# Attention loads issued later, first keys earlier, and weight conversion steps moved in a fused attention and two-layer MLP kernel

## The chip, the cores and the metric

The kernel runs on one NeuronCore of a Trainium2 chip. The metric is device time in microseconds of one execution. 1076.02 us is the median of three runs before the change. A profile was taken of one more execution. The engines are called as the profile calls them: PE (matmul, PEld for its weight loads), DVE (VectorE), ACT (ScalarE), POOL (GpSimd), SP (SyncE, which here issues nearly all loads and stores; SPq is its queue).

## The reference

Chunked attention with a few memory keys, then two products of gated linear layers. Cut to what matters:

```python
batch, n_heads, seq, head_dim = (4, 8, 768, 64); n_mem = 8
chunk, left_ctx, right_ctx = (32, 16, 8)
for c in range(seq // chunk):
    k_full = concat([mem_k, k[l_start:r_end]]); v_full = concat([mem_v, v[l_start:r_end]])
    a = softmax(scale * q_c @ k_full.T)
    out[c] = a @ v_full
x = out as (3072 tokens, 512)
a = x @ w1; b = x @ w2              # 512 -> 1024
x = ((a * b) @ w3) @ w_out          # 1024 -> 1024 -> 512
y = ((x @ w_a) * (x @ w_b)) @ w_out2   # 512 -> 1536 -> 512
```

## The kernel before, in words

The work is one long stream of matmuls on PE in four stages, written out in an order that Python fixes; the other engines run what is queued to them, in order.

Stage 1 multiplies w3 by w_out once (tiles wps, lines 566 to 605), in two halves of 16 steps g; each step is two matmuls of 128 x 512, and four banks of results are evicted to wo by w_evict at the end of a half (ACT writes the high part, DVE the low part). The weights come as 64-bit words, and are made into 32-bit floats on the way: SP loads a raw block (w_load, line 350; w3a and w3b blocks of 1 MiB, w12 blocks of 0.5 MiB), ACT scales its two halves (w_scale, line 366, two instructions, L372 and L373), DVE adds them (w_bits, L377 and L378), and for w12 blocks ACT writes the high part (L414) and DVE the low part (L408). A call of w_tick moves this pipe by a step: w_turn does the later stages of the blocks in it, w_next scales the next block and loads as many blocks as there are free buffers. A buffer is free when its block's sum is done. The numbers of g after which a tick is called are tables in the loop.

Stage 2 is attention, in 16 groups u of 192 tokens, laid into the matmul stream in slots: attn_slot runs what the table todo holds for the next slot. A group starts at slot BASE[u] and has these steps, each a few slots after the one before: a_scores (PE, tile sc, from the queries q and the widened keys kw), a_max and a_exp (DVE and ACT, tile t), a_norm (DVE, then POOL), a_trans (PE, tile pt), a_pt (ACT copies it to p), a_pv (PE, tile xp, with the values v), a_x (ACT and DVE split it into the high and low part of xt). pt and xp share one PSUM buffer, so that the transpose of a group waits for the xt of the group before. There is one buffer each for kraw, kw, q and v: a_k loads kraw, a_keys widens it into kw, a_q loads q once the scores of the group before are through, a_v loads v once the value product of the group before is through. Slot 0 is in step g 9 of the first half, slot 7 is g 0 of the second.

Stage 3 runs x @ w1 and x @ w2 (psA, psB) in blocks of 512 tokens, the gate (g) and the product with wo (psY), with the remaining groups of attention in between. Stage 4 is the last layer.

SP's queue is in program order: a load that waits (for its buffer, say) holds up all loads behind it.

Of the kernel before, what the change touches and what calls it, by code (L numbers as in the profile page):

```python
# [45 lines left out]
def tile_attention_moe(  # L46
# [42 lines left out]
    def mm(o, l, r, first, last):  # L89
        nc.tensor.matmul(o, lhsT=l, rhs=r, start=first, stop=last)  # L90
# [16 lines left out]
    def new_batch(u):  # L107
        return NE * u % NG == 0

    def a_k(u):  # L110
        if u >= NA:
            return
        k = ks[u] = att.tile([P, NE, 4 * KW], F32, tag="kraw", bufs=1, name="kraw")
        src = kt[2 * NE * u, D : 2 * D].rearrange("d h k -> d (h k)")
        row, x = src.ap
        step = 2 * 2 * D * row[0]
        src = bass.AP(src.tensor, src.offset, [[row[0], P], [step, NE], x])
        nc.sync.dma_start(out=k, in_=src)

    def a_q(u):  # L120
        if u >= NA:
            return
        q = qs[u] = att.tile([P, NE, 4 * GQ], F32, tag="q", bufs=1, name="q")
        src = qt[2 * NE * u : 2 * NE * u + 2 * NE]
        nc.sync.dma_start(
            out=q, in_=src.rearrange("(e r) d h q -> (r d) e (h q)", r=2)
        )

    def a_v(u):
        if u >= NA:  # L130
            return
        for r in range(2):
            for e in range(NE):
                src = vw[2 * NE * u + 2 * e + r]
                kd, x = src.ap
                if new_batch(u):
                    mem = bass.AP(src.tensor, src.offset, [[kd[0], NMEM], [0, NC], x])
                    nc.sync.dma_start(out=v[D * r : D * r + NMEM, e, :, :], in_=mem)
                win = bass.AP(
                    src.tensor,  # L140
                    src.offset + NMEM * kd[0],
                    [[kd[0], KEYS - NMEM], [CHUNK * kd[0], NC], x],
                )
                nc.sync.dma_start(out=v[D * r + NMEM : D * r + D, e, :, :], in_=win)

    def a_keys(u):
        if u >= NA:
            return
        k = ks.pop(u).rearrange("p e (h k) -> p (e h) k", h=4)
        p, a, e = k.ap  # L150
        win = bass.AP(
            k.tensor, k.offset + NMEM * e[0], [p, a, [CHUNK * e[0], NC], [e[0], KEYS - NMEM]]
        )
        nc.vector.tensor_copy(kw[:, :, :, NMEM:], win)
        if new_batch(u):
            nc.vector.tensor_copy(
                kw[:, :, :, 0:NMEM], k[:, :, None, 0:NMEM].to_broadcast([P, NH, NC, NMEM])
            )
# [37 lines left out]
    def a_exp(i):  # L196
        def stage_of(u):
            sc, t, mx, sm = soft[u]
            for a in range(2 * i, 2 * i + 2):
                for r in range(2):  # L200
                    nc.scalar.activation(  # L201
                        t[:, a, r, :],
                        sc[:, r, a, :],
                        AF.Exp,
                        bias=mx[:, r, a : a + 1],
                        scale=SCALE,
                        accum_out=sm[:, a, r : r + 1],
                    )

        return stage_of  # L210

    def a_norm(e):
        def stage_of(u):
            t, mx, sm = soft[u][1:]
            t, sm = t[:, 4 * e : 4 * e + 4], sm[:, 4 * e : 4 * e + 4]
            nc.vector.tensor_scalar_add(sm, sm, 1e-9)
            nc.vector.reciprocal(sm, sm)  # L217
            nc.gpsimd.tensor_tensor(  # L218
                t, t, sm[:, :, :, None].to_broadcast([GQ, 4, 2, KEYS]), ALU.mult
            )  # L220

        return stage_of
# [52 lines left out]
    BASE = [0, 6, 13, 23, 29, 36]  # L275
# [5 lines left out]
    def at(s, *stages):  # L281
        todo.setdefault(s, []).extend(stages)

    for u in range(NA):
        t0, t1, t2, t3 = SLOTS.get(u, (6, 7, 8, 9) if u < NX else (5, 5, 6, 7))
        for s, stage_of in (
            (t0, a_trans),
            (t1, a_pt),
            (t3, a_x),
            (t2, a_pv),  # L290
            (t2, lambda u: a_v(u + 1)),
            (0, a_scores),
            (0, lambda u: a_q(u + 1)),
            (int(u > 0), a_max),
            (2, a_norm(0)),
            (2 + (u > 0), a_norm(1)),
            (int(u > 0), a_exp(0)),
            (int(u > 0), a_exp(1)),
            (2 * (u > 0), a_exp(2)),
            (2 * (u > 0), a_exp(3)),  # L300
        ):
            at(BASE[u] + s, (stage_of, u))
        if u > 0:
            at(BASE[u] - 3, (a_keys, u), (a_k, u + 1))
    at(0, (a_v, 0))
    NEED = []
    for i in range(NT1):
        u = -(-TT * (i + 1) // (NE * GQ)) - 1
# [3 lines left out]
    def attn_slot(n=1):  # L312
        for _ in range(n):
            s = acount[0]
            if s >= NEED[-1]:
                return
            acount[0] += 1
            for stage_of, u in todo.get(s, []):
                stage_of(u)
# [84 lines left out]
    def w_turn():  # L404

        if len(pipe[2]):
            i, a, ax, (d, f, w, hi, lo) = pipe[2].pop(0)
            nc.vector.tensor_tensor(lo, a, hi.bitcast(F32), ALU.subtract)  # L408
            live["dec"][ax] -= 1
            d[f] = w  # L410
        if pipe[1]:
            i, a, ax = pipe[1].pop(0)
            t = w_place(*plan[i][:3])
            nc.scalar.activation(t[3], a, AF.Copy)  # L414
            pipe[2].append((i, a, ax, t))
        if len(pipe[0]):
            i, r, tag = pipe[0].pop(0)
            a, ax = w_sum(i, r)
            live[tag][int(tag == "raw2")] -= 1
            if ax is not None:  # L420
                pipe[1].append((i, a, ax))

    def w_next():
        if wraw:
            i, r, tag = wraw.pop(0)
            for (r1,) in pieces_of(i, r):
                w_scale(r1)
            pipe[0].append((i, r, tag))
        while w_load():
            pass  # L430

    def w_tick():
        w_turn()
        w_next()
# [126 lines left out]
    def w_evict(half, m):  # L561
        w = wsm[4 * half + m] = w_new(wpool, "wo")
        nc.scalar.activation(w[:, 0, :], banks[m], AF.Copy)
        nc.vector.tensor_tensor(w[:, 1, :], banks[m], w[:, 0, :].bitcast(F32), ALU.subtract)

    for half in range(2):
        banks = [psd.tile([P, 512], F32, tag="d", name="wps") for _ in range(4)]
        for k in range(8):
            for m in range(4):
                mm(  # L570
                    banks[m],
                    w3k[8 * half + k].bitcast(F32)[:, P * m : P * m + P],
                    wo_f[k].bitcast(F32),
                    k == 0,
                    k == 7,
                )
                if k == 7 and m > 0:
                    w_evict(half, m - 1)
                if m % 2 == 0:
                    continue  # L580
                g = 2 * k + m // 2
                if half == 0:
                    if g >= 9:
                        attn_slot()
                    if g in (0, 2, 4, 6, 8, 9):
                        w_tick()
                    if g == 2:
                        a_k(0)
                        a_q(0)
                    if g == 7:  # L590
                        a_keys(0)
                        a_k(1)
                    if g == 9:
                        bound[0] = len(wsrc)
                    if g == 15:
                        w_turn()
                else:
                    attn_slot()
                    if g == 0:
                        w_next()  # L600
                    if g in (1, 2, 3, 4, 5, 9, 10, 11):
                        w_tick()
        w_evict(half, 3)
    del pairs["f"]
# [425 lines left out]
```

## Time and profile before

| | us |
|---|---|
| median of three runs | 1076.02 (1075.88 to 1077.11) |
| profiled execution, its own time | 1074.61 |
| its span in the profile | 1072.8 |
| PE busy in the span | 1055.9 (98%) |
| PEld, DVE, ACT, POOL busy | 844.5, 452.1, 443.3, 233.3 |

A busy share is the share of the span in which an engine has an instruction at work. Behind an instruction the views give in brackets how long its engine stood idle before it and which instruction (engine, tile, line) ended that wait. A wait for several things is put down to the one that came last. Matmuls of 32-bit floats appear as two records each.

### The profile page before, as it was taken

Reading aid. Unit: us, or ns where it says so; the run is one execution under the profiler, and the core shown is the slowest. Engines: PE = TensorE matmul, PEld = TensorE weight load, DVE = VectorE, ACT = ScalarE, POOL = GpSimd, SP = SyncE. Lnnn points to the kernel's source line nnn. Section 1 sums busy time; section 2 is a strip of 40 time slices with the busy share of each in tenths; the row PEclk is TensorE's granted clock in tenths of the full one; section 3 lists DMA queues with packets and bytes.
Section 4 is the critical chain, followed back from the end, with each engine's and each line's share of the span. In section 5 each row is a group of like instructions: output and inputs, shape, how many; then the busy total and the mean of one; then the engine's idle time right before and its main releaser. Section 6 shows DMA issues by size and latency. Waiting matters only on the chain.

```text
span 1072.8 us, 18442 instructions
## 1 busy us (share of the span) xinstructions
PE 1055.9 (98%) x7442; PEld 844.5 (79%) x7442; DVE 452.1 (42%) x751; ACT 443.3 (41%) x1153; POOL 233.3 (22%) x228
## 2 busy tenths in 40 slices
PE   9999899999999999999999999999999999999998
PEld 3447688888888888888888888888888888888886
DVE  4667644435435435346643434432322253223310
ACT  6777754426636543535433343332222232222210
POOL 0102312202303302212033222112233202222210
PEclk9999999999999999999999999999999999999999
DMA  9966464454454462263555554523344434433311
GB/s 366 315 174 185 132 186 142 130 164 149 150 187 116 141 188 91 104 235 138 196 200 210 202 182 158 186 97 148 137 151 178 158 111 141 172 139 138 137 40 39
DMA packets 62341, 172.02 MB, mean 160 GB/s; under 512 B 6320, under 2 KB 21552, under 8 KB 56368
## 3 DMA queue, kind: packets, MB, share of 16 engines
q1 hardware_dynamic: 51680, 104.75, 30.2%
q0 software_dynamic: 10368, 66.06, 17.0%
q8 instruction: 58, 0.95, 0.4%
q14 instruction: 27, 0.22, 0.1%
q10 hardware_dynamic: 208, 0.04, 0.0%
HBM read 137.27 MB, written 33.55 MB: 159 GB/s over the span
## 4 chain that ended last, share of the span: by engine, by line
PE 86%; DVE 1%; DMA 1%; ACT 0%; issue 0%; POOL 0%; SPq 0%; ACTq 0%; POOLq 0%
PE ps L816 31%; PE ops L90 18%; PE psY L90 12%; PE psB L90 11%; PE psA L90 10%; PE xp L90 2%; PE sc L90 1%; PE pt L229 1%; DMA raw<-in_wab 1%; DVE x L102 0%; DVE tmp L670 0%; POOL g L635 0%; ACT x L99 0%; POOL t L218 0%; DVE xt L102 0%
## 5 line engine op out<-in xcount | busy, mean ns | idle before, releaser
L816 PE MATMUL ps<-x,w 128*128 128x512 f32 x1512 | 348.7, 389 | 0.3 <-ACT tmp L828 0.3
L816 PEld LDWEIGHTS ps<-x,w 128*128 128x128 f32 x1512 | 283.6, 188 | 60.1 <-ACT tmp L828 1.4
L833 DVE TENSOR_TENSOR tmp<-ps,tmp 128x512 f32<-128x512 f32 x108 | 74.6, 691 | 260.7 <-PE ps L816 230.6
L90 PE MATMUL psA<-xt,w 128*128 128x512 f32 x576 | 140.9, 393 | 3.8 <-DVE w L408 3.0
L90 PE MATMUL psB<-xt,w 128*128 128x512 f32 x576 | 140.0, 392 | 0.0
L90 PE MATMUL psY<-g,wo 128*128 128x512 f32 x576 | 136.0, 392 | 0.3 <-POOL g L635 0.3
L635 POOL TENSOR_TENSOR g<-gv,g 128x512 fp32r<-128x512 f32 x48 | 65.0, 1354 | 301.5 <-ACT g L634 301.5
L828 ACT ACTIVATE tmp<-ps 128x512 f32<-128x512 f32 x108 | 64.5, 597 | 157.5 <-PE ps L816 157.5
L90 PEld LDWEIGHTS psA<-xt,w 128*128 128x128 f32 x576 | 107.0, 188 | 28.0 <-DVE w L408 3.8
L90 PEld LDWEIGHTS psY<-g,wo 128*128 128x128 f32 x576 | 107.0, 188 | 23.1 <-POOL g L635 0.8
L90 PEld LDWEIGHTS psB<-xt,w 128*128 128x128 f32 x576 | 107.2, 188 | 22.5
L700 POOL DMA_DIRECT2D w<-wc x72 | 39.6, 552 | 373.3 <-PE ps L816 373.2
L90 PE MATMUL ops<-wo,g 128*128 128x512 f32 x504 | 118.6, 389 | 0.0
L90 PEld LDWEIGHTS ops<-wo,g 128*128 128x128 f32 x504 | 94.6, 188 | 19.6
L839 ACT ACTIVATE g<-tmp 128x512 fp32r<-128x512 f32 x66 | 40.7, 633 | 140.2 <-DVE tmp L838 140.2
L840 POOL TENSOR_TENSOR g<-tmp,g 128x512 fp32r<-128x512 f32 x66 | 84.0, 1291 | 20.8 <-ACT g L839 19.7
L201 ACT ACTIVATE t<-sc,mx 96x64 f32<-96x64 f32 x256 | 75.3, 316 | 25.0 <-DVE mx L193 23.4
L90 PE MATMUL ops<-fo,g 128*128 128x512 f32 x288 | 68.2, 389 | 0.0
L90 PEld LDWEIGHTS ops<-fo,g 128*128 128x128 f32 x288 | 54.1, 188 | 11.2
L218 POOL TENSOR_TENSOR t<-t,sm 96x512 f32<-96x512 f32 x32 | 37.2, 1163 | 104.6 <-DVE sm L217 100.3
L90 PE MATMUL wps<-w_f 128*128 128x512 f32 x128 | 57.6, 600 | 1.9 <-DVE w_f L378 1.9
L201 ACT ACTIVATION_READ_ACCUMULATOR t<-sc,mx 96x1 f32 x256 | 53.9, 211 | 0.0
(65 smaller groups left out, 870.3 us busy)
## 6 DMA issues: line engine op xcount, KB each, us to landing
w<-wc POOLq DMA_DIRECT2D x36, 1024.0 KB, 7.0
w<-wc POOLq DMA_DIRECT2D x36, 768.0 KB, 5.1
wc<-co SPq DMA_DIRECT2D x84, 256.0 KB
raw<-in_wab SPq DMA_DIRECT2D x24, 512.0 KB
v<-in_vw SPq DMA_DIRECT2D x64, 168.0 KB
kraw<-in_kt SPq DMA_DIRECT2D x16, 512.0 KB
raw<-in_w SPq DMA_DIRECT2D x16, 512.0 KB
raw<-in_w3a SPq DMA_DIRECT2D x6, 1024.0 KB
```

The lines of the kernel that those rows point to most:

```text
L90: nc.tensor.matmul(o, lhsT=l, rhs=r, start=first, stop=last)
L201: nc.scalar.activation(t[:, a, r, :], sc[:, r, a, :], AF.Exp, bias=mx[:, r, a : a + 1], scale=SCALE, accum_out=sm[:, a, r : r + 1],)
L218: nc.gpsimd.tensor_tensor(t, t, sm[:, :, :, None].to_broadcast([GQ, 4, 2, KEYS]), ALU.mult)
L229: nc.tensor.transpose(pt[:, a // 4, a % 4, :], t[:, a].rearrange("p r k -> p (r k)"), id_sb)
L635: nc.gpsimd.tensor_tensor(g2[:, 1, :], gv, g2[:, 0, :].bitcast(F32), ALU.subtract)
L700: nc.gpsimd.dma_start(out=t[:, c0:c1].bitcast(F32), in_=src[:, c0:c1])
L816: nc.tensor.matmul(ps, lhsT=w[:, i, a, k, :], rhs=xs[i][:, b, k, :], start=first and n == 0, stop=n == 5, skip_group_check=not first,)
L828: nc.scalar.activation(z, ps, AF.Copy)
L833: nc.vector.tensor_tensor(z, ps, y, ALU.add)
L839: nc.scalar.activation(g2[:, 0, :], z, AF.Copy)
L840: nc.gpsimd.tensor_tensor(g2[:, 1, :], z, g2[:, 0, :].bitcast(F32), ALU.subtract)
```

## The change

a_q and a_v of the next group are queued one or two slots later, a_k one slot later. The first keys and queries are loaded at g 0, not g 2. The last w_turn of the first half is at g 13, not 15. In the second half the ticks at g 2 and 3 go to 6 and 12 (each number names the slot after which it is: the list 1, 2, 3, 4, 5, 9, 10, 11 becomes 1, 4, 5, 6, 9, 10, 11, 12).

```diff
-            (t2, lambda u: a_v(u + 1)),
             (0, a_scores),
-            (0, lambda u: a_q(u + 1)),
...
         if u > 0:
-            at(BASE[u] - 3, (a_keys, u), (a_k, u + 1))
+            at(BASE[u] - 3, (a_keys, u))
+            at(BASE[u] - 2, (a_k, u + 1))
+        at(BASE[u] + 1 + (u > 0), (a_q, u + 1))
+        at(BASE[u] + t2 + 1 + (u > 1), (a_v, u + 1))
     at(0, (a_v, 0))
...
-                    if g == 2:
+                    if g == 0:
                         a_k(0)
                         a_q(0)
...
-                    if g == 15:
+                    if g == 13:
                         w_turn()
...
-                    if g in (1, 2, 3, 4, 5, 9, 10, 11):
+                    if g in (1, 4, 5, 6, 9, 10, 11, 12):
                         w_tick()
```

Lines behind the first piece move down by one (L357 becomes L358).

The order on SP, from the last loads of w3a on. Before:

```order
L357 DMA raw_156<-in_w3a 128x2048
L357 DMA raw_166<-in_w3a 128x2048
L118 DMA kraw<-in_kt 128x2x512
L125 DMA q<-in_qt 128x2x384
L357 DMA raw_181<-in_w3b 128x2048
L357 DMA raw_191<-in_w3b 128x2048
L118 DMA kraw<-in_kt 128x2x512
L357 DMA raw_206<-in_w3b 128x2048
L125 DMA q<-in_qt 128x2x384
L138 DMA v<-in_vw 8x3x256
L144 DMA v<-in_vw 56x3x256
L138 DMA v<-in_vw 8x3x256
```

With the change the same queue begins

```order
L358 DMA raw_156<-in_w3a 128x2048
L118 DMA kraw<-in_kt 128x2x512
L125 DMA q<-in_qt 128x2x384
L358 DMA raw_170<-in_w3a 128x2048
L358 DMA raw_181<-in_w3b 128x2048
```

and goes on, from the second group's keys, with

```order
L118 DMA kraw<-in_kt 128x2x512
L358 DMA raw_206<-in_w3b 128x2048
L138 DMA v<-in_vw 8x3x256
L144 DMA v<-in_vw 56x3x256
L138 DMA v<-in_vw 8x3x256
L144 DMA v<-in_vw 56x3x256
L138 DMA v<-in_vw 8x3x256
L144 DMA v<-in_vw 56x3x256
L138 DMA v<-in_vw 8x3x256
L144 DMA v<-in_vw 56x3x256
L358 DMA raw_293<-in_w3b 128x2048
L125 DMA q<-in_qt 128x2x384
```

The first kraw and q stand one raw load earlier; the second group's q went from ahead of the first group's eight v loads to behind them and behind the raw load that follows.

The order on ACT in the first steps of the second half (t is the exponentials of the second group, xt the split of the first). Before:

```order
L201 ACTIVATE t,sm<-sc,mx 96x64 x8
L372 ACTIVATE raw_206<-raw_206 128x1024
L373 ACTIVATE raw_206<-raw_206 128x1024
L372 ACTIVATE raw_295<-raw_295 128x1024
L373 ACTIVATE raw_295<-raw_295 128x1024
L99 ACTIVATE xt<-xp 128x4x192
```

Now:

```order
L201 ACTIVATE t,sm<-sc,mx 96x64 x8
L373 ACTIVATE raw_206<-raw_206 128x1024
L374 ACTIVATE raw_206<-raw_206 128x1024
L99 ACTIVATE xt<-xp 128x4x192
L373 ACTIVATE raw_293<-raw_293 128x1024
L374 ACTIVATE raw_293<-raw_293 128x1024
```

One scale pair has gone from ahead of the split to behind it.

The order on DVE around the xt of the second group, from its step's normalization on (dec is the sum of a w12 block). Before:

```order
L408 TENSOR_TENSOR w_534<-dec,w_534 128x512
L377 TENSOR_SCALAR dec<-raw_420 128x512
L378 ISA dec<-raw_420,dec 128x1024
L102 TENSOR_TENSOR xt<-xp,xt 128x4x192
L408 TENSOR_TENSOR w_534<-dec,w_534 128x512
```

Now:

```order
L378 TENSOR_SCALAR dec<-raw_416 128x512
L379 ISA dec<-raw_416,dec 128x1024
L102 TENSOR_TENSOR xt<-xp,xt 128x4x192
L409 TENSOR_TENSOR w_671<-dec,w_671 128x512
L378 TENSOR_SCALAR dec<-raw_418 128x512
L379 ISA dec<-raw_418,dec 128x1024
```

The third w12 block (raw_420 before, raw_418 now) is summed behind the xt subtraction and a low half, not ahead of them.

## Rows read from the trace of the kernel before

**Rows 1.** PE's waits: what for, us in total, times, longest.

```profile
PE pt L229 <- DVE xt L102: 2.5, 1, 2.5
PE wps L90 <- DVE w_f L378: 1.9, 3, 1.3
PE sc L90 <- DVE kw L156: 1.5, 1, 1.5
...
PE psY L90 <- POOL g L635: 0.3, 1, 0.3
```

**Rows 2.** Timeline of PE: start, duration, instruction, idle before it.

```profile
40.22 1.18 PE L90 MATMUL sc<-kw,q 64*32 64x64 f32 x96
...
57.50 0.85 PE L229 MATMUL pt<-id_sb,t 96*128 96x96 f32 x8 [2.50 <-DVE xt L102]
...
77.50 1.60 PE L90 MATMUL xp<-p,v 64*64 64x32 f32 x96
```

**Rows 3.** Timeline of SP's queue, stage 1.

```profile
30.08 0.39 SPq L125 DMA_DIRECT2D q<-in_qt  x1
...
38.27 0.27 SPq L138 DMA_DIRECT2D v<-in_vw  x1
40.10 0.32 SPq L144 DMA_DIRECT2D v<-in_vw  x1
40.52 0.36 SPq L357 DMA_DIRECT2D raw<-in_w3b  x1
...
71.53 0.35 SPq L357 DMA_DIRECT2D raw<-in_w  x1
```

**Rows 4.** SP's waits between 25 and 45 us.

```profile
SPq L138 <- DMA raw<-in_w3b: 3.8, 2, 3.2
...
SPq L144 <- DMA kraw<-in_kt: 1.9, 1, 1.9
SPq L144 <- DMA q<-in_qt: 1.5, 1, 1.5
```

**Rows 5.** GB/s moved by DMA in 40 slices of the span.

```profile
GB/s 366 315 174 185 132 186 142 130 164 149 150 187 116 141 188 91 104 235 138 196 200 210 202 182 158 186 97 148 137 151 178 158 111 141 172 139 138 137 40 39
```

**Rows 6.** Timeline of ACT in the second half of stage 1.

```profile
53.48 1.20 ACT L372 ACTIVATE raw<-raw 128x1024 f32<-128x1024 f32 x1
...
55.53 0.83 ACT L99 ACTIVATE xt<-xp 128x768 fp32r<-128x768 f32 x1
...
68.41 0.67 ACT L414 ACTIVATE w<-dec 128x512 fp32r<-128x512 f32 x1
...
70.06 0.82 ACT L99 ACTIVATE xt<-xp 128x768 fp32r<-128x768 f32 x1
...
75.24 0.68 ACT L372 ACTIVATE raw<-raw 128x512 f32<-128x512 f32 x1 [0.46 <-DMA raw<-in_w]
...
76.40 0.80 ACT L235 ACTIVATE p<-pt 128x768 f32<-128x768 f32 x1
```

**Rows 7.** Timeline of DVE in the second half of stage 1.

```profile
56.40 0.96 DVE L102 TENSOR_TENSOR xt<-xp,xt 128x768 fp32r<-128x768 f32 x1 [1.32 <-ACT xt L99]
...
72.25 0.68 DVE L408 TENSOR_TENSOR w<-dec,w 128x512 fp32r<-128x512 f32 x1
...
74.03 0.68 DVE L408 TENSOR_TENSOR w<-dec,w 128x512 fp32r<-128x512 f32 x1
```

**Rows 8.** PE's last matmuls, and the program's end by windows (PEclk is the granted clock).

```profile
1062.22 5.60 PE L90 MATMUL ops<-wo,x 128*128 128x512 f32 x24
...
1069.00:1070.00 1.00, 0.00 (x0) 0.00 (x0) 0.00 (x0) 0.00 (x0) 0.00 (x0) 1.00 1.02 379
...
1071.00:1072.00 1.00, 0.00 (x0) 0.00 (x0) 0.00 (x0) 0.00 (x0) 0.00 (x0) 0.50 0.00 0
```

**Rows 9.** Timeline of the first matmuls and their weight loads.

```profile
1.46 6.42 PE L90 MATMUL warm<-wz 96*96 96x512 f32 x10 [1.46 <-DVE wz L549]
...
4.98 0.28 PEld L90 LDWEIGHTS warm<-wz 96*96 96x96 f32 x1 [0.57 <-issue]
...
6.00 0.16 PEld L90 LDWEIGHTS warm<-wz 96*96 96x96 f32 x1 [0.27 <-issue]
```

## The prediction

> **What bounds the kernel now.** I read PE's waits first. PE is the engine that sets the end, and nearly all of the span it is at work, so only a wait of PE's own can be won or lost, and there are few [rows 1]: 2.5 us before a transpose (pt) for the split of an attention group into xt, 1.9 us in three waits for decoded weights (w_f), the longest 1.3, 1.5 us for the first keys (kw), and 0.3 us late in the first token block for g. The timeline of PE [rows 2] places them. The second group's scores run at 40.22 with no wait in their row, the 1.3 us for w_f comes right behind them, the transpose of the second group starts at 57.50 after 2.50 idle, and the third group's value product starts at 77.50 without a wait.
>
> Second, the SP queue, since most of the diff is about loads [rows 3]. The second group's queries are issued at 30.08, the last of the first group's eight value loads only at 40.10, and the next weight load 0.42 us behind it, at 40.52. Why the value loads crawl stands in SP's own waits [rows 4]: one waited 3.2 us for raw weights from w3b, one 1.9 us for keys, one 1.5 us for queries. None of these shares a buffer with v. Counting back along the queue, each waited for the load issued eight places ahead of it: SP doesn't issue a load until the one eight before has landed. So raw_206 landed at 38.27, and the second queries at 40.10, 0.1 us before PE used them at 40.22 [rows 2, 3]. That margin is what the forecast turns on.
>
> **The change part by part.**
>
> First keys. kraw and q now go ahead of one 1 MiB raw load. At the 366 GB/s of the first slice [rows 5], 1.05 MB is 2.9 us, more than PE's 1.47 us wait, and the raw load that is pushed back feeds weights that PE wants only two steps of k later. Gain 1.47 us (bounds 0 and 1.47). PE then reaches the second group's scores at 40.22 - 1.47 = 38.75.
>
> The w_turn of the first half goes from g 15 to g 13, ahead of the evictions on DVE. The w_f it makes is then there before PE asks. Gain 1.30 us (bounds 0 and 1.30). The evictions are pushed back by less than this one sum.
>
> The two ticks taken out of the gap: on ACT the xt split of the first group stands ahead of the last w3b scale pair, not behind it. It started at 55.53, and DVE's subtraction, 0.96 long from 56.40, ended 0.14 us before the transpose [rows 2, 6, 7]. The pair that goes from in front took 53.48 to 55.53, 2.05 us [rows 6]. On DVE the maximum of the second scores is no longer behind an eviction and a w_f sum either, so the exponentials on ACT start sooner. I take all 2.50 us as gained (bounds 2.05 and 2.5).
>
> Second queries. Here the change costs. a_q(1) moves from slot 0 to slot 1, and a_v(0) and a tick now come ahead of it: in SP's order it stands behind eight value loads and the 1 MiB raw_293. The eighth value load still waits for the load eight places ahead, now raw_206. The loads ahead of raw_206 are the same as before, so it lands at about 38.0 as before (38.27). Then v at 38.0, raw_293 at 38.4, q at 38.8. PE wants it at 38.75, so all of its flight is a PE wait. The flight: a 0.5 MiB load issued at 71.53 on a quiet queue was taken by ACT at 75.24, so 3.71 us [rows 3, 6]; the other half of raw_293 and q itself are 0.92 MB, 2.5 us at 366 GB/s [rows 5]; from 38.4 that is 44.6. The lower bound is 3.71 us after q's own issue, 42.5, as if raw_293 cost nothing. The upper is what this same load took before, 10.0 us from 30.08 to 40.10 [rows 3], so 48.8. I take 45.0, nearest to the worked-out value and a little to the loaded side. Loss 45.0 - 38.75 = 6.25 us (bounds 3.7 and 10). While PE waits, DVE and ACT can't go on with the second group either, so what follows is shifted whole.
>
> The Trainium skill's DMA: Bandwidth & Descriptors (Anatomy of one DMA) gives, fitted for loads issued from GpSimd, 2.0 us plus bytes at 436 GB/s: for the 1.44 MB of both loads an estimate of 5.3 us, landing at 43.7, and the sum below would be 1.3 us smaller. The trace's 10.0 us for the one load stands against so short a flight under load. Its section Rules for kernel authors says to issue a load early and wait for it late, which speaks against this edit.
>
> The clock. PE would stand still for 6.25 us; it has never waited over 2.5. The nearest row is the end of the program: the last matmul ends at 1067.82, the granted clock is 1.00 (2.4 GHz) in 1069 to 1070 and 0.50 (1.2 GHz) in 1071 to 1072 [rows 8]. So I expect it to fall here. The nearest price is the start: the warm-up matmuls began at 1.46, their weight loads take 0.28 us at 4.98 and 0.16 us at 6.00 [rows 9], so nearly 4 us of work passed at the low level and half of it was lost. I take 1.8 us (bounds 0 and 2).
>
> The later ticks. The third w12 block's sum stood ahead of the second group's xt subtraction on DVE; now it stands behind it. Its buffer is what the sixth block's load waits for, that block's scale stands on ACT ahead of the copy of p, and PE's value product needs p. Before: exponentials done at 68.41, load at 71.53, scale at 75.24, copy at 76.40, product at 77.50 [rows 2, 3, 6], that is 9.1 us from the exponentials' end. Now: xt split after 1.65 (70.06 - 68.41), subtraction 0.87 later and 0.87 long until the next starts, a low half and a sum 1.78 (72.25 to 74.03) [rows 6, 7], so the load goes out after 5.2; flight 3.71, scale 1.16, copy 0.80: 10.9. PE is then 1.8 us late, and 0.8 more because a sum of twice the width now stands ahead of the group's maximum: 2.6 us lost (bounds 0, if PE comes late for another reason, and 4, if the flight is a microsecond longer).
>
> Attention loads a slot or two later, further on: keys, queries and values have four to six slots until they are used, and PE there waits for none of them [rows 1]. Zero. They free SP's queue: the first wab loads no longer stand behind a q that waits for PE, so the 0.33 us for g goes (bounds 0 and 0.33).
>
> Sum: -1.47 - 1.30 - 2.50 - 0.33 + 6.25 + 1.8 + 2.6 = +5.05 us. The profiled execution took 1074.61, so 1079.7. The median of the runs, 1076.02, is 1.41 above that execution; with the same difference, **1081.1**.
>
> **The rivals.**
>
> Clock holds. All as above without the 1.8 us: 1079.3. For it: no wait in the trace is so long in mid-program. Against: the tail [rows 8].
>
> p is not late. PE arrives at the third value product as late as ACT: without the 2.6 us, 1078.5, and if the clock holds as well, 1076.7.
>
> Queries half late. The flight is near its lower bound and q lands between 41 and 43: with the clock kept and p late, 1075.3 to 1077.3, no difference to be seen.
>
> Faster: the queries come in time. If SP doesn't hold the eighth value load until raw_206 has landed (the waits of rows 4 being for something else), q goes out near 31 and is there for PE. Then neither the 6.25 nor the 1.8 us arise, and the gains less p's 2.6 us leave -3.0: 1073.0, or 1070.4 if p isn't late either. Its place is SP between 29 and 39 us. It decides at a landing of 41.75: earlier the kernel is faster, later slower (clock kept). For it: the waits removed are all plain in rows 1. Against: three rows of SP, each with the right load eight places ahead.
>
> The edits cancel or the waits only move: 1076.
>
> **How the numbers follow.** A measurement of this kernel can tell about 0.2%, 2.15 us, from no change. Forecast 0.47, clock holds 0.20, p not late 0.10 (half of it within 0.2%), half late or cancelled 0.09, in time 0.11, worse than all bounds of the forecast 0.03. Slower by over 0.2%: 0.47 + 0.20 + 0.05 + 0.03 = 0.75. Within: 0.05 + 0.09 = 0.14. Faster: 0.11. The range leaves out the faster case and the worst tail: from 1076.0 (half late) to 1084.0 (q at 46.5 and p's load a microsecond longer).
>
> **What would show it.** In PE's waits after: none for kw and w_f at these places, pt's 2.5 gone, and a new one of about 6 us for q ahead of the second group's scores near 39; SP issues that q at 38 to 39, after the eighth v. PE's clock at 0.50 somewhere from 39 to 50. A wait of 2 to 3 us ahead of the third group's value product, ended by ACT's p. The forecast is wrong if the second scores start before 42, or if SP issues the second queries before 36.

## The result and the profile after

The changed kernel takes 1086.17 us (median of four runs, 1084.96 to 1086.94) against 1076.57 for the kernel before (four runs, the three above and one more): a ratio of 1.0085, 95% interval 1.0069 to 1.0102. It is slower, as forecast, but by 9.6 us where 5.05 were forecast, and 1086.17 lies outside the range of 1076.0 to 1084.0. The profiled execution of it took 1084.96, with a span of 1083.2, 10.4 above the 1072.8 of the profiled execution before.

PE's waits in the changed kernel (what for, us in total, times, longest), to be read against [rows 1]:

```profile
PE sc L90 <- DMA q<-in_qt: 6.9, 1, 6.9
PE xp L90 <- ACT p L235: 5.4, 1, 5.4
PE psA L90 <- DVE w L409: 3.0, 2, 2.2
...
PE psA L90 <- DVE xt L102: 0.5, 1, 0.5
PE wps L90 <- DVE w_f L379: 0.4, 2, 0.2
```

The waits that the change was aimed at are gone: kw's 1.5, pt's 2.5, psY's 0.3, and of w_f's 1.9 only 0.4 is left. Two new ones took their place, for the second queries and for the third group's exponentials (p). The psA wait of 3.0 for w is not new: the kernel before has it too, at the same size (3.0 in two waits, the longer 2.2).

The timeline of PE (start, duration, instruction, idle before it and what ended it) places them, against [rows 2]:

```profile
37.78 0.83 PE L229 MATMUL pt<-id_sb,t 96*128 96x96 f32 x8
45.54 1.95 PE L90 MATMUL sc<-kw,q 64*32 64x64 f32 x96 [6.94 <-DMA q<-in_qt]
47.42 6.71 PE L90 MATMUL wps<-w_f 128*128 128x512 f32 x12
...
60.85 0.83 PE L229 MATMUL pt<-id_sb,t 96*128 96x96 f32 x8
...
86.34 2.79 PE L90 MATMUL xp<-p,v 64*64 64x32 f32 x96 [5.44 <-ACT p L235]
89.06 2.94 PE L90 MATMUL wps<-w_f 128*128 128x512 f32 x4
```

Not only the waits cost. Behind each the same instructions run longer than before. The weight products of the kernel before in these two places:

```profile
42.71 5.42 PE L90 MATMUL wps<-w_f 128*128 128x512 f32 x12 [1.30 <-DVE w_f L378]
...
79.03 1.98 PE L90 MATMUL wps<-w_f 128*128 128x512 f32 x4
```

(The views count two records for each matmul, and the counts of scores, value products and weight products in this text are those of the views.) The 96 scores took 1.95 us (1.18 in [rows 2]), the twelve weight products 6.71 (5.42 before), the value product 2.79 (1.60 in [rows 2]), the last four weight products 2.94 (1.98 before). Why, the windows of the same trace say (stretch, its length, busy us and count of PE, PEld, DVE, ACT, POOL; then PE's granted clock, DMA share, GB/s):

```profile
38.00:40.00 2.00, 0.61 (x8) 0.42 (x6) 2.00 (x5) 1.39 (x2) 0.00 (x0) 1.00 0.22 54
40.00:42.00 2.00, 0.00 (x0) 0.00 (x0) 0.59 (x1) 0.00 (x0) 0.00 (x0) 1.00 0.95 294
42.00:44.00 2.00, 0.00 (x0) 0.00 (x0) 0.00 (x0) 0.00 (x0) 0.00 (x0) 0.81 0.96 390
44.00:46.00 2.00, 0.46 (x29) 0.49 (x35) 0.00 (x0) 0.00 (x0) 0.00 (x0) 0.50 1.08 407
...
78.00:80.00 2.00, 2.00 (x6) 0.88 (x5) 1.66 (x3) 1.07 (x2) 0.00 (x0) 1.00 1.09 245
80.00:82.00 2.00, 0.90 (x3) 0.07 (x1) 1.53 (x3) 0.69 (x2) 0.00 (x0) 1.00 1.13 199
82.00:84.00 2.00, 0.00 (x0) 0.00 (x0) 0.00 (x0) 0.00 (x0) 0.00 (x0) 1.00 0.97 362
84.00:86.00 2.00, 0.00 (x0) 0.00 (x0) 0.00 (x0) 1.60 (x3) 0.00 (x0) 0.55 1.01 396
```

Two things stand here. The clock falls from 1.00 (2.4 GHz) to 0.50 (1.2 GHz) twice, once in each wait; in the trace of the kernel before it was 1.00 through all of this, in the same places too:

```profile
42.00:44.00 2.00, 1.29 (x3) 0.68 (x4) 2.00 (x3) 0.00 (x0) 0.00 (x0) 1.00 0.92 341
...
84.00:86.00 2.00, 2.00 (x99) 1.53 (x100) 0.97 (x2) 0.60 (x1) 0.00 (x0) 1.00 0.44 99
```

And between 38 and 40 us the DMA engines are nearly idle (share 0.22, 54 GB/s) while PE already wants the queries: they were issued only at 39.70. The SP queue in the two places, against [rows 3]:

```profile
38.83 0.32 SPq L144 DMA_DIRECT2D v<-in_vw  x1
39.24 0.36 SPq L358 DMA_DIRECT2D raw<-in_w3b  x1
39.70 0.40 SPq L125 DMA_DIRECT2D q<-in_qt  x1
...
73.96 0.34 SPq L358 DMA_DIRECT2D raw<-in_w  x1
74.39 1.72 SPq L144 DMA_DIRECT2D v<-in_vw  x4
...
76.88 0.36 SPq L358 DMA_DIRECT2D raw<-in_w  x1
```

SP's longest wait for a load between 20 and 50 us (what for, us in total, times, longest), against [rows 4]:

```profile
SPq L144 <- DMA raw<-in_w3b: 7.1, 2, 4.0
```

The 4.0 us end at 38.83: the eighth value load stood there until raw_206, eight places ahead of it, was through. And ACT, which takes the two w12 blocks and then makes p (the first row starts where the exponentials of the third group end), against [rows 6]:

```profile
71.55 0.67 ACT L415 ACTIVATE w<-dec 128x512 fp32r<-128x512 f32 x1
...
78.93 0.68 ACT L373 ACTIVATE raw<-raw 128x512 f32<-128x512 f32 x1 [1.44 <-DMA raw<-in_w]
...
84.40 0.65 ACT L373 ACTIVATE raw<-raw 128x512 f32<-128x512 f32 x1 [3.71 <-DMA raw<-in_w]
...
85.50 0.79 ACT L235 ACTIVATE p<-pt 128x768 f32<-128x768 f32 x1
```

The queries are issued at 39.70, behind the eighth value load and raw_293, and PE has them at 45.5. The sixth w12 block is issued at 76.88 and taken at 84.40: a flight of 7.52 us for a load that took 3.71 before (71.53 to 75.24, [rows 3, 6]). Four value loads went out right ahead of it (74.39 to 76.11), and the fifth block, issued at 73.96, was still in flight until about 78.93.

### The profile page after: what moved, and what is told of

It is laid out like the page before. It is cut to its first block, busy times and chain, and to the rows that moved or that the text cites. A ratio compares the mean times of both kernels' runs of the same rounds, so it can differ in the third digit from the quotient of the medians.

```text
span 1083.2 us, 18436 instructions
## 1 busy us (share of the span) xinstructions
PE 1059.9 (98%) x7442; PEld 847.2 (78%) x7442; DVE 451.8 (42%) x751; ACT 443.5 (41%) x1153; POOL 233.4 (22%) x228
## 4 chain that ended last, share of the span: by engine, by line
PE 86%; DVE 1%; ACT 0%; issue 0%; ACTq 0%
PE ps L817 31%; PE ops L90 18%; PE psY L90 12%; PE psB L90 11%; PE psA L90 11%; PE xp L90 2%; PE sc L90 1%; PE pt L229 1%; DVE x L102 0%; DVE tmp L671 0%; ACT x L99 0%; DVE kw L154 0%; DVE w L409 0%; DVE tmp L834 0%; ACT tmp L893 0%
## 5 line engine op out<-in xcount | busy, mean ns | idle before, releaser
L90 PE MATMUL wps<-w_f 128*128 128x512 f32 x128 | 59.8, 619 | 0.4 <-DVE w_f L379 0.4
L635 ACT ACTIVATE g<-gv 128x512 fp32r<-128x512 f32 x48 | 30.4, 634 | 59.8 <-DVE gv L634 59.8
```

The lines of the kernel that those rows point to most:

```text
L635: nc.scalar.activation(g2[:, 0, :], gv, AF.Copy)
```

## The experiments

Diffs are against the changed kernel where nothing else is said. Eight of the runs are a single execution each; the other four are medians of ten. The first four below stand beside 1077.21 us for the kernel before, the later ones beside its median of 1075.68 (the wait filled, the values from GpSimd) or 1076.01 (the two edits together, the loads alone), each of nineteen runs. Both sets of nineteen lie between 1073.86 and 1077.88, so a single time that differs by 2 us or less decides nothing by itself; there the rows have to.

**Queries first.** The second queries go back to slot 0, ahead of the value loads.

```diff
-        at(BASE[u] + 1 + (u > 0), (a_q, u + 1))
+        at(BASE[u] + 2 * (u > 0), (a_q, u + 1))
```

> The changed kernel, with one thing put back: the second group's queries are queued in slot 0 again, ahead of the first group's eight value loads. Order theory (the queries are late because the eighth value load waits for the load eight places ahead, raw_206, and the queries and raw_293 come behind it): SP issues them near 28, they land about 1 us after raw_206, at 39.5 to 40.2, and PE's wait for q falls from 6.94 us to 1 to 1.5. The clock then doesn't fall at 43, which gives back another 2 us; the wait for p before the third value product stays at about 5, with its fall of the clock. In all 7 to 8 us less than the changed kernel: about 1077 to 1078.5. Rival (the load queues are so full at this time that the queries land late wherever they stand): the wait stays over 4 us and the time within 3 us of the changed kernel's.

1080.97 us. The queries' wait fell from 6.94 to 1.91, so the place in the queue is the cause of the other five. The time came down by 5.2, less than expected: the 5 us wait for p stayed, as expected, and the clock fell all the same, behind a wait of 1.91, which was not.

```profile
40.61 1.19 PE L90 MATMUL sc<-kw,q 64*32 64x64 f32 x96 [1.91 <-DMA q<-in_qt]
41.72 7.11 PE L90 MATMUL wps<-w_f 128*128 128x512 f32 x12
```

**Queries behind the values, ahead of the weights.** Only raw_293, 1 MiB, is taken from in front of the queries.

```diff
-        at(BASE[u] + 1 + (u > 0), (a_q, u + 1))
+        if u > 0:
+            at(BASE[u] + 2, (a_q, u + 1))
...
     at(0, (a_v, 0))
+    at(0, (a_q, 1))
```

> The changed kernel, with the second group's queries queued in slot 0 but behind the eight value loads: only raw_293 goes from ahead of them. Order theory: SP still issues them only when raw_206 has landed, at 39.2 to 39.4 (39.70 in the changed kernel), and they land some 3.5 to 4 us later, at 42.8 to 43.3; PE's wait is 4 to 4.5 us, about 2.5 less than the 6.94. Rival (raw_293 ahead of them is the whole cause): the wait falls to about 1, as in the kernel with the queries first. Rival (full queues): 6 to 7 us as before.

1083.3 us. SP issued the queries at 39.47, only 0.23 sooner, as the eighth value load still went out at 39.05; yet the wait was 4.28, 2.66 shorter, as the order theory had it. So raw_293 ahead of the queries costs 2.7 us of the wait, 2.4 of them in flight (5.84 us from issue to the scores' start, now 3.40); the prediction's working had it at 2.1 (44.6 less 42.5). And against the run before it the place behind the values costs 2.4 (4.28 - 1.91).

**Ticks back.** The old list of ticks in the changed kernel.

```diff
-                    if g in (1, 4, 5, 6, 9, 10, 11, 12):
+                    if g in (1, 2, 3, 4, 5, 9, 10, 11):
```

> The changed kernel with the old list of ticks (1, 2, 3, 4, 5, 9, 10, 11), the later value loads kept. Theory (p is late because the sixth w12 block's load goes out late and behind the third group's four value loads, so that it takes 7.5 us): the sixth block's load goes out ahead of the value loads, its flight is under 5 us, PE's wait of 5.44 us for p falls under 1, and the clock doesn't fall a second time, 7 us less; but the transpose of the second group waits for xt again, 0 to 2 us (it was 2.50). The wait for q stays at 6 to 7. In all 5 to 7 us less than the changed kernel: 1078 to 1081. Rival (the value loads one slot later are enough to make p late, whatever the ticks): the wait for p stays over 3.

1084.51 us, where 1078 to 1081 were expected. The wait for p went from 5.44 to 1.17 (the sixth block, issued at 76.13 just ahead of the values, was taken at 81.38, a flight of 5.25), but the value product then stops after its first matmul (two records) for the values themselves, 0.69, and the clock falls there all the same, so that little is won:

```profile
83.33 0.30 PE L90 MATMUL xp<-p,v 64*64 64x32 f32 x2 [1.17 <-ACT p L235]
84.31 2.78 PE L90 MATMUL xp<-p,v 64*64 64x32 f32 x94 [0.69 <-DMA v<-in_vw]
```

The transposes waited 0.93 here, not 2.50: with PE held up earlier by the queries, the split into xt is late by less even with the old ticks.

**Third group's values a slot sooner.** One edit, meant for the four value loads that stand ahead of the sixth block's load.

```diff
-        at(BASE[u] + t2 + 1 + (u > 1), (a_v, u + 1))
+        at(BASE[u] + t2 + (u != 1) + (u > 1), (a_v, u + 1))
```

> The changed kernel with only the third group's value loads one slot sooner, as before the change; they then go out ahead of the fifth w12 block's load, not between the fifth and the sixth. The first part of the theory alone (the load is late by a tick: 2.6 us as forecast; the rest of the 5.44 is the value loads right ahead of it): the sixth block's flight falls from 7.5 to 3.7 to 5 us, PE's wait for p to 1.5 to 3 us, and the clock doesn't fall there: 4.5 to 6 us less than the changed kernel, 1079.5 to 1082. Rival (the late ticks alone make it): wait and flight stay, and so does the time, within 2 us.

1080.52 us, 5.65 below the changed kernel. The four value loads now went out from 71.82 on, ahead of the fifth block's load, and the sixth block was issued at 77.14 and taken at 82.16: a flight of 5.02. The wait for p is 2.15, and there is no second fall. That 2.15 is near the 2.6 of the prediction is luck: the flight is 1.3 us longer than the forecast's, and the third group's exponentials end 7.4 us after its scores start (64.40 to 71.81), a microsecond sooner than before (8.4), where the forecast had them 0.8 later. PE's rows:

```profile
84.10 1.60 PE L90 MATMUL xp<-p,v 64*64 64x32 f32 x96 [2.15 <-ACT p L235]
85.63 1.98 PE L90 MATMUL wps<-w_f 128*128 128x512 f32 x4
```

**The wait filled with work.** Seven matmuls in the place where PE waits for the queries.

```diff
+        if u == 1:
+            for _ in range(7):
+                mm(sc[:, 0, :], w3k[0].bitcast(F32)[:, :GQ], wo_f[0].bitcast(F32), True, True)
```

> This run adds seven matmuls of 128x512 (about 0.86 us each, 6.0 us in all) ahead of the second group's scores; their result is overwritten, so the output is the reference's. They lie in the 6.94 us in which TensorE waits there for the second queries. Theory that the clock falls at 43 us because TensorE stands still in that wait: the wait shrinks to about 1 us, the clock holds 2.4 GHz through 44 to 50, the scores take 1.20 instead of 1.95 and the weight products 5.42 instead of 6.71 us, and the span is about 2 us shorter (time about 1083); the wait for the exponentials (5.44) and the second fall at 84 stay. Rival, that the fall has to do with what follows the wait (the scores and the transposes): the low stretch stays, only later, and the time is 1085 to 1086.

1085.81 us. The queries' wait was 0.60, the clock stood at 1.00 from 36 to 58, and the scores and twelve weight products took 1.18 and 5.42. So it is PE's standing still that takes the clock there: the time is the rival's, the rows are the theory's. The 2 us did not reach the end. PE came to the third value product 2 us sooner, and waited longer:

```profile
85.64 2.79 PE L90 MATMUL xp<-p,v 64*64 64x32 f32 x96 [6.81 <-ACT p L238]
88.36 3.65 PE L90 MATMUL wps<-w_f 128*128 128x512 f32 x4
```

The sixth block was taken at 83.70, only 0.70 sooner: the load sets the time there, not PE. Even the 0.70 is lost again: behind this longer wait the clock is low from about 81.5 to 91 us (84 to 91 in the changed kernel), and it falls once more from 136 to 139.5, where the trace of the changed kernel has 1.00.

**The same with the third group's values a slot sooner.** The two edits above together.

```diff
+        if u == 1:
+            for _ in range(7):
+                mm(sc[:, 0, :], w3k[0].bitcast(F32)[:, :GQ], wo_f[0].bitcast(F32), True, True)
...
-        at(BASE[u] + t2 + 1 + (u > 1), (a_v, u + 1))
+        at(BASE[u] + t2 + (u != 1) + (u > 1), (a_v, u + 1))
```

> The change with the third group's values a slot sooner (the run that took the exponentials' wait from 5.44 to 2.15 us at 1080.5) and with the seven added matmuls in the second queries' wait, which leave the output as it is. Theory that the first fall of the clock costs about 2 us, which in the run with the added matmuls alone was swallowed by the exponentials' wait (6.8 for 5.44): here, where that wait is shorter, at least half of it shows, 1078 to 1079.5, with the clock at 2.4 GHz from 42 to 52. Rival, that the block's load sets the time again: the exponentials' wait grows by as much as the clock gives back, and the time stays at 1080 to 1081.

1077.45 us, 3.07 below the run with the value loads alone (1080.52). The clock stood at 1.00 in all the windows from 36 to 156 us; in the run without the added matmuls it is at 0.50 from 42 to 52, and there the scores took 1.95 and the weight products 7.58 us, 2.93 more than 1.18 and 5.42 here. The wait for p grew by only 0.46. So in this pair the fall of the clock costs 3 us, where no load hides it. By the same two rows the first fall costs 2.06 in the changed kernel, and 1.7 (queries first) to 2.9 (values from GpSimd) in the other runs that have it.

**The eight values from GpSimd's queue.** In a_v the eight loads of the first group, those ahead of the second queries on SP, are issued by nc.gpsimd, the rest by nc.sync. (The expectation calls them the second group's.)

```diff
+        eng = nc.gpsimd if u == 0 else nc.sync
...
-                    nc.sync.dma_start(out=v[D * r : D * r + NMEM, e, :, :], in_=mem)
+                    eng.dma_start(out=v[D * r : D * r + NMEM, e, :, :], in_=mem)
...
-                nc.sync.dma_start(out=v[D * r + NMEM : D * r + D, e, :, :], in_=win)
+                eng.dma_start(out=v[D * r + NMEM : D * r + D, e, :, :], in_=win)
```

> The eight value loads of the second group are issued from GpSimd's queue, everything else as in the change. Theory that the queries come late because SP holds each load back until the load eight places ahead of it has landed: SP issues the queries at about 31.5 instead of 39.7, they land at about 41 to 42.5, TensorE waits 2.5 to 4 us for them instead of 6.94, and the time is 1081 to 1084. Rival, that the DMA engines have no room before 45 whoever issues: issued early, the queries still land at 44 to 45, the wait stays at 6 to 7 us and the time at 1084 to 1086. The wait for the exponentials (5.44) is expected to stay with both.

1085.79 us, and it decides nothing. GpSimd issued these loads from 1.4 us on, and the whole start moved: the weight load that SP issued at 15.72 in the changed kernel came at 19.00, and PE's transposes at 42.01, not 37.78. The queries went out at 36.81, not 31.5, and PE had them at 45.97, later than in the changed kernel. PE's wait for them, 3.13, lies in the theory's range only because PE came 4 us later. That SP's order alone makes them late is not shown by this run.

**Keys and conversion alone.** The kernel before with a_k(0), a_q(0) at g 0 and w_turn at g 13, nothing else (diff against the kernel before).

```diff
-                    if g == 2:
+                    if g == 0:
...
-                    if g == 15:
+                    if g == 13:
```

> The kernel before with only the sooner first keys and queries and the sooner last conversion of the first weights (the part of the change that moves no later load and no tick). The prediction's terms for these are -1.5 and -1.3 to -1.5 us. Theory that they are real gains which the loads then bury: 1072.5 to 1073.5, with TensorE's wait for the first transposes (2.5) and the one before the second half (0.3) left as before. Rival, that they move the second queries' loads and are lost there: 1075 to 1077.

1074.64 us (ten runs; before 1076.01), ratio 0.9991, 0.9981 to 1.0002: no gain that can be told from none, and between the two expectations. PE's waits say where the gain stuck:

```profile
PE pt L229 <- DVE xt L102: 2.2, 1, 2.2
PE sc L90 <- DMA q<-in_qt: 1.7, 1, 1.7
```

kw's 1.5 is gone, and 1.7 for the second queries stands in its place: the scores start at 40.25, as before (40.22, [rows 2]). The queries went out at 27.39, 2.7 us sooner than before, and landed no sooner. The margin of 0.1 us that the prediction saw there held back the first keys' gain by itself, with no later load moved. What the moved w_turn gains does show in the trace: no wait for w_f is left, and the third value product starts at 75.82, 1.7 us sooner than in [rows 2].

**Ticks alone.** The kernel before with the new list of ticks (diff against the kernel before).

```diff
-                    if g in (1, 2, 3, 4, 5, 9, 10, 11):
+                    if g in (1, 4, 5, 6, 9, 10, 11, 12):
```

> The kernel before with only the new ticks (1,4,5,6,9,10,11,12 for 1,2,3,4,5,9,10,11). Theory: the wait of 2.5 us for the first transposes goes, and as the value loads stand where they stood, the sixth block's load is late by less than the forecast's 2.6 us, so that the exponentials cost 0.5 to 2.6: 1073 to 1076.5. Rival, that the ticks alone make the exponentials 5 us late, with or without the value loads ahead of them: 1078 to 1081.

1077.73 us (ten runs), ratio 1.0019, 1.0009 to 1.0029: slower. The wait for the transposes fell to 0.41, and the one for p became 2.68. Here the values stand where they stood, out from 65.06 on; the sixth block was issued at 72.15 and taken at 75.89, a flight of 3.74. Those are the prediction's 3.71 and 2.6 almost to the tenth, and its steps hold as well: the exponentials end 9.2 us after the scores start (57.64 to 66.82, 8.4 before, so 0.8 later as forecast), and the load goes out 5.3 us behind them (5.2 forecast). The time lies above the expectation's upper end, 1076.5; in the profiled execution the clock fell behind that wait, where four weight products took 3.60 us (1.98 before), and again from 127 to 131 us. The rows of the first place:

```profile
77.87 1.60 PE L90 MATMUL xp<-p,v 64*64 64x32 f32 x96 [2.68 <-ACT p L235]
79.40 3.60 PE L90 MATMUL wps<-w_f 128*128 128x512 f32 x4
```

**Loads alone.** The kernel before with only the later keys, queries and values (diff against the kernel before).

```diff
-            (t2, lambda u: a_v(u + 1)),
...
-            (0, lambda u: a_q(u + 1)),
...
-            at(BASE[u] - 3, (a_keys, u), (a_k, u + 1))
+            at(BASE[u] - 3, (a_keys, u))
+            at(BASE[u] - 2, (a_k, u + 1))
+        at(BASE[u] + 1 + (u > 0), (a_q, u + 1))
+        at(BASE[u] + t2 + 1 + (u > 1), (a_v, u + 1))
```

> The kernel before with only the later attention loads (keys, queries, values), ticks and conversions as before. Theory that these loads carry nearly all of the loss: the second queries' wait is 6 to 7.5 us, the clock falls once behind it (1 to 2.5 us), the wait for the first transposes is 0 to 2.5, and the time is 1082 to 1086. Rival, that the loss needs the new ticks as well: 1077 to 1081.

1082.98 us, 7 above the kernel before. The queries' wait is 5.82, a little less than expected, the one for p 0.97 (the sixth block flew 5.06, 76.28 to 81.34), for the values 0.57; the transposes wait 0.71 for xt even here, with the old ticks; and the clock falls in two places, from 44 and from 84 us on, not in one. The loads carry most of the loss without any other part of the change.

**The parts set right.** Queries at slot 0, the first groups' values where they stood, ticks moved less; first keys and conversion as in the change.

```diff
-        at(BASE[u] + 1 + (u > 0), (a_q, u + 1))
-        at(BASE[u] + t2 + 1 + (u > 1), (a_v, u + 1))
+        at(BASE[u] + 2 * (u > 0), (a_q, u + 1))
+        at(BASE[u] + t2 + (2 if u > 1 else 0), (a_v, u + 1))
...
-                    if g in (1, 4, 5, 6, 9, 10, 11, 12):
+                    if g in (1, 4, 5, 6, 7, 9, 10, 11):
```

> The change with the queries a slot sooner (as in the run with the queries first), the values of the first groups where the kernel before has them, and weight-load ticks 1,4,5,6,7,9,10,11; the sooner first keys and the moved conversions stay. Theory of three prices: the queries' wait is about 1.9 us, no wait for the exponentials over 1.5 us, none for the first transposes over 1 us, and the gains of the change (1.5 + 1.5 + 2.5 + 0.3) stay: 1072 to 1076, below the kernel before, if the clock holds; with one fall of the clock 1074 to 1078. Rival, that the sooner queries push the weight loads and bring the late exponentials back (5 us): 1079 to 1082.

1074.03 us (ten runs; before 1075.68 in nineteen), ratio 0.9984, 0.9975 to 0.9993: a little faster than the kernel before, by 1.65 us, and 12 us faster than the change. What is left to wait for:

```profile
PE sc L90 <- DMA q<-in_qt: 1.9, 1, 1.9
PE warm L90 <- DVE wz L550: 1.5, 1, 1.5
PE pt L229 <- DVE xt L102: 1.5, 1, 1.5
PE xp L90 <- ACT p L235: 0.5, 1, 0.5
```

The 1.5 for xt is the third group's transposes (71.25); the second group's, which the change was aimed at, wait no more.

**The same with two matmuls in the queries' wait.** The diff of the version above, and with it

```diff
+        if u == 1:
+            for _ in range(2):
+                mm(sc[:, 0, :], w3k[0].bitcast(F32)[:, :GQ], wo_f[0].bitcast(F32), True, True)
```

> As the run before it, with two matmuls of 128x512 (1.7 us, result overwritten) added ahead of the second group's scores, in the wait for the queries. Theory that standing still there costs the clock: the wait is under 0.5 us, the clock holds through 42 to 52, and the time is 1 to 2.5 us below that of the run without them, if that one falls there; if that one's clock holds, the two are equal within 0.5 us. Rival, that the added work only lengthens the path: 1 to 1.7 us slower.

1074.03 us (ten runs; against the kernel before a ratio of 0.9981, 0.9971 to 0.9990): equal to the version without them. The added work took 1.88 us, the queries' wait of 1.88 was gone, and the scores started at 40.36 where they had started at 40.39. The clock had held at 1.00 there without it.

## Why the prediction was right and wrong

**Right: the gains, as rows.** kw, pt and psY are gone from PE's waits, w_f is down by 1.5 (1.30 forecast). But three of the reasons were not whole. The transposes' wait shrinks to 0.71 to 0.93 with the old ticks too, once PE is held up by the queries (loads alone, ticks back); the ticks alone take it to 0.41. And the first keys, set at 1.47, are worth nothing by themselves, as the second queries land at 40.1 to 40.6 whether PE is there or not (before, keys and conversion alone, queries first, parts set right). The 0.33 for g, which the prediction put down to the later loads, is gone with keys and conversion alone too, where no later load moved.

**Right: the queries.** 6.94 measured, 6.25 forecast, with the mechanism as written: SP's eighth value load waits until raw_206 has landed, then raw_293 and q follow. Issue 39.70 (38.8 forecast), landing 45.5 (45.0). The two runs that move the queries show its two halves: raw_293 ahead of them costs 2.7 us, their place behind the values 2.4; the last 1.9 stay even with the queries first, since PE is there sooner. The rows' working gave raw_293 and the queries 6.2 us together (38.4 to 44.6); they took 6.3 (39.24 to 45.54). By the page DMA: Bandwidth & Descriptors of the Trainium skill (Anatomy of one DMA), which the prediction gave beside it, they would take an estimated 5.3. Issued at 27.57, 12 us sooner, the queries' load costs PE 1.9 us and not 6.9. The rule of that page of the Trainium skill to issue a load early and wait for it late (Rules for kernel authors) agrees. The load lands only 5 us sooner, though, at about 40.5: the DMA engines stood at full share in that run in every window of 2 us from 10 to 38 us (0.96 to 1.11).

**Wrong: the term "the later ticks", 2.6 us, measured 5.44.** Its chain was right, and with it the size for the ticks alone (2.68, flight 3.74). What failed is the flight of 3.71 us, read from a load with a quiet queue, and the sentence that the attention loads further on cost zero. Before, the third group's values went out from 67.45 to 69.39, 2 us ahead of the sixth block's load, and the fifth block's load long before them. The same diff moves these values a slot later, and with the later ticks the fifth block's load, the values and the sixth block's load go out within 3 us (73.96 to 76.88); the sixth then flies 7.52 us. The whole of it takes both: the flight is 3.74 with the ticks alone, 5.06 with the loads alone and 5.25 with the ticks back. Its upper bound of 4 ("if the flight is a microsecond longer") was too low by the same fault. A single edit that moves these values out from between them brings the flight to 5.02 and the wait to 2.15. The other part of the term, 0.8 for exponentials that end later, did not come in the changed kernel: they end 8.2 us after the scores start (63.35 to 71.55), 8.4 before. So the flight cost 3.8 more than forecast, and this gave about 1 back.

**Wrong: the term "the clock", 1.8 us for one fall.** There were two falls, and by the rows they cost 4.2 us: 0.77 and 1.29 behind the first (scores, weight products), 1.19 and 0.96 behind the second (value product, weight products). The first alone, 2.06, is near the 1.8 and just over the upper bound of 2; in other runs it was up to 2.9. What failed is the count. The second stands in the wait for p, and the run in which that wait is 2.15 has only the first; but the length of that wait alone does not decide it, since the clock falls there too with 2.68 (ticks alone) and with 1.17 and 0.69 (ticks back).

The sum by rows of the two profiled executions is then -1.5 (kw) - 1.5 (w_f) - 2.5 (pt) - 0.3 (psY) + 6.9 (q) + 5.4 (p) + 4.2 (clock) = +10.7, against 10.4 between the spans. These prices are not what each cause is worth alone: with the first fall taken away, nothing was won (1085.81), as the sixth block's load set the time behind it and the clock was low for longer there; with the values moved as well, taking it away won 3 us.

Measured one part at a time, keys and conversion give -1.4, ticks +1.7, loads +7.0, in all +7.3, and the whole change +9.6. The 2.3 between them would be what ticks and loads do together, late values between two block loads, and the flights above show that there is such a thing. But I did not run that pair without the other parts, and the loads alone are a single execution of a time that spreads over 4 us in the kernel before, so the size of 2.3 is not shown.

**Left open.** Why the clock falls after some short waits and not after others. It was 1.00 behind the 2.50 of [rows 2] and behind the 1.88 of the version with the parts set right, and fell behind the 1.91 of the run with the queries first, at nearly the same instant. In the profiled execution of the version with the parts set right it falls between 124 and 130 us, behind two waits of 0.74 and 2.23; that of the kernel before has the same two (0.77 and 2.23) without a fall. Nor does the kernel alone seem to decide it: of that version's ten executions, two with a mean clock of 0.999 took 1072.25 and 1072.60 us, and eight with 0.997 or 0.998 took 1073.82 to 1074.77, which fits a fall of about 1.5 us that some executions are spared. The run that filled the wait shows that PE's standing still is a cause; how little of it is enough, no run here settles.

## What to carry to other kernels

Before a load is moved in a queue, list for every load behind it what flies beside it, and take its flight from a row with the same neighbours, not from a quiet one. A margin of 0.1 us at a load's landing means that whatever makes its user come sooner gains nothing until that load is sooner too. And price a long new wait of PE at the wait, plus the slower work behind it, plus what a chain of loads will hide or add further on.

## What the hardware showed that I had not expected

While the small value loads fly, the DMA engines are full and move fewer bytes. The four are 168 KB each, 0.69 MB in all, in rows of 1 KB (256 elements of f32). In the windows from 78 to 82 us above, the engines stand at shares of 1.09 and 1.13 and move 245 and 199 GB/s; from 82 us on they move 362 and 396. In the run with the ticks back the same step has the values' arrival beside it: 212 GB/s at a share of 1.04 from 82 to 84 us, PE goes on with the values at 84.31, and from 84 to 86 it is 360 at 1.02. By bytes the four would be 1.9 us at the 366 GB/s of [rows 5]; the sixth block's flight grew by 3.8, and the 0.52 MB of the fifth block, still in flight, are at most 1.4 of that. That the short rows are the reason fits, but no run here changed the rows' length, and a value load fills 56 partitions where a block fills 128, which no run tells apart from it.

Filling a wait cost nothing here: 1.88 us of added matmuls in a wait of 1.88 left the time where it was, and 6.17 us in the 6.94 kept the clock at 2.4 GHz.
